# Packed dense convolutions for the first three blocks, a band built from tiny fp16 matmuls, weights loaded in thirds, and a new order of the first casts, moves and loads

## The chip, the cores and the metric

One core of one Trainium2 chip. The metric is device microseconds of one execution. A program on one core has no second die to compare with, but each run lists its span (first to last instruction) and its mean granted TensorE clock. A single number below is a median over the runs named beside it.

## The reference, cut to what matters

```python
# x: (8, 4160, 192) fp32; weight: (8, 7); w1, w2, w3: (192, 768); w_out: (768, 192)
w = softmax(weight, axis=-1)                       # 8 heads, 7 taps
conv[b, s, h*24 + g] = sum_k w[h, k] * x_padded[b, s + k, h*24 + g]   # causal, 6 zeros ahead
h = max(conv @ w1, conv @ w2, conv @ w3)
out = h @ w_out
```

The 33,280 tokens are worked through in 65 blocks of 512. The kernel uses max(a, b, c) = max(relu(a - c), b - c) + c: layer 1 computes the two differences with `w1 - w3` and `w2 - w3`, and the term in `c` is carried by a product `m = w3 @ w_out`.

## The kernel before: the parts that the argument touches

The first two blocks use a "dense" conv, straight from a spread-out copy of x (`xz`). All later blocks use a packed conv from `x16`, whose result is then moved into place by six small DMA moves (`repack`) and one DMA that doubles it onto the other 64 partitions (`double`). In the cuts, `l1(t, j)` is layer-1 step j of block t, `st2` the output stage, `evac` copies a conv's result out of the matmul's memory, and `keep_warm(n)` issues n idle matmuls on zeros, whose result nobody reads, so that TensorE does not stand still.

```python
    # the band of taps: broadcast by a matmul, softmax on 128 partitions,
    # seven products on VectorE, seven matmuls that sum them
    keep_warm(2)
    nc.tensor.matmul(wps..., lhsT=ones[:], rhs=wk[:], ...)
    ...
    for k in range(KW):
        nc.vector.tensor_mul(out=shifted[:, k, :, :], in0=<unit, shifted by k>, in1=<tap k>)
    keep_warm(7)
    for k in range(KW):
        nc.tensor.matmul(ps[:], lhsT=ident16[:], rhs=shifted[:, k, :, :], ...)
    keep_warm(3)
    ...
    def repack(t):                       # six moves, three of them on the sync queue
        for n, (half, s0, c, r0, rows) in enumerate(pieces):
            (nc.sync, nc.gpsimd)[n % 2].dma_start(out=yd[r0:r0 + rows, c, :],
                                                  in_=slots[t][s0:s0 + rows, half, :])

    def double(t):
        nc.sync.dma_start(out=dense[t][HALF:P, :, :], in_=dense[t][0:HALF, :, :])
    ...
    for t in range(1, NB):
        u = t + AHEAD                    # AHEAD = 3
        load_x(t + 7)                    # sync queue
        cast_x(t + 5)                    # GpSimd, needs load t+5
        double(u - 1)                    # sync queue
        begin(t)
        l1(t, 0)
        ...  conv(u) [and conv(u + 1) in even blocks], evictions
        repack(u)
        st2(t - 1, 0, NJ)                # first sixth of the output stage of block t-1
        ...
```

All `load_x`, all `double` and half of the moves share one in-order queue, that of the sync engine. What waits there holds everything behind it: in the trace of the kernel before, the doublings wait there 124 times for moves to land, 184.8 us in all.

The softmax here doesn't subtract the row's maximum and nothing guards it: scores larger than these inputs give would overflow.

## Time and profile before

| | before |
|---|---|
| median (range) | 480.11 us (479.98 to 480.84, 3 runs) |
| span of the profiled run | 479.2 us (that run: 481.05) |
| busy TensorE | 468.5 us, 9083 matmuls |
| block 2 begins | 34.09 us |
| two steady blocks | 13.95 us |

The lines that carry this are in the prediction.

### The profile page before, as it was taken

The numbers are of one execution on the slowest core, as the hardware profiler recorded it, in microseconds if no ns is written. First come the engines' busy times: TensorE is split into PE (matmuls) and PEld (weight loads), VectorE is DVE, ScalarE is ACT, GpSimd is POOL, SyncE is SP. The second block draws the span as 40 slices with busy tenths as digits, with TensorE's granted clock in tenths as the row PEclk, the third lists the DMA queues.
The fourth block names the chain that finished last, engine by engine and source line by source line (L and its number), as shares of the span: only waits on it lengthen the run. The fifth ranks groups of instructions, "written<-read, shape, count | busy, mean of one in ns | idle before, by whom it ended". The sixth has DMA issues, their size and how long they took to land.

```text
span 479.2 us, 21943 instructions
## 1 busy us (share of the span) xinstructions
PE 468.5 (98%) x9083; PEld 393.6 (82%) x9083; DVE 366.2 (76%) x609; ACT 327.2 (68%) x608; POOL 211.0 (44%) x340
## 2 busy tenths in 40 slices
PE   7899999999999999999999999999999999999996
PEld 3468888888888888888888888888888888888995
DVE  6667777877777787777778777877877787787775
ACT  5666766767676676767676676767667676766664
POOL 2555435543543454354345434534535453454200
PEclk9899999999999999999999999999999999999999
DMA  8958756656666665666666666665656755644313
GB/s 188 230 150 221 205 168 188 179 178 178 191 173 175 169 187 172 174 190 176 172 186 171 177 171 179 187 173 171 183 162 177 212 165 168 181 139 122 98 67 100
DMA packets 68035, 82.08 MB, mean 171 GB/s; under 512 B 9440, under 2 KB 56272, under 8 KB 67936
## 3 DMA queue, kind: packets, MB, share of 16 engines
q1 hardware_dynamic: 54478, 49.41, 41.0%
q0 software_dynamic: 13104, 30.98, 18.4%
q8 instruction: 71, 1.16, 1.1%
q10 hardware_dynamic: 354, 0.30, 0.2%
q14 instruction: 28, 0.23, 0.1%
HBM read 30.31 MB, written 25.56 MB: 117 GB/s over the span
## 4 chain that ended last, share of the span: by engine, by line
PE 97%; ACT 1%; DVE 1%; issue 1%; POOL 0%; POOLq 0%
PE lp L383 32%; PE po L426 30%; PE lq L383 26%; PE G L322 7%; PE D L342 1%; PE idle L196 1%; PE band_sum L245 0%; ACT band L268 0%; ACT w3h L262 0%; ACT r L387 0%; DVE xz L216 0%; DVE h L388 0%; PE pm L301 0%; PE wps L223 0%; PE pm L305 0%
## 5 line engine op out<-in xcount | busy, mean ns | idle before, releaser
L388 DVE TENSOR_TENSOR h<-r,lq 128x512 f16<-128x512 f16 x390 | 267.2, 686 | 101.6 <-ACT r L387 101.6
L387 ACT ACTIVATE r<-lp 128x512 f16<-128x512 f32 x390 | 232.9, 597 | 136.1 <-PE lp L383 90.2
L383 PE MATMUL lp<-yd,wd 64*128 64x512 f16 x1170 | 315.8, 377 | 0.2 <-DVE wd L254 0.2
L383 PE MATMUL lq<-yd,wd 64*128 64x512 f16 x1170 | 315.0, 375 | 0.2 <-DVE h L388 0.2
L426 PE MATMUL po<-wo,h 64*128 64x192 f16 x3120 | 231.4, 243 | 0.0
L426 PEld LDWEIGHTS <-h 64*128 64x128 f16 x3120 | 187.2, 94 | 25.6
L383 PEld LDWEIGHTS <-wd 64*128 64x128 f16 x2340 | 164.4, 94 | 21.4 <-issue 1.7
L452 POOL DMA_DIRECT2D out_dram<-o x63 | 50.1, 795 | 240.0 <-DVE o L436 223.2
L366 POOL DMA_DIRECT2D yd<-ys x189 | 95.7, 511 | 2.2 <-ACT ys L353 1.6
L426 PE MATMUL po<-m,yd 64*128 64x192 f16 x780 | 87.0, 243 | 0.0
L436 DVE TENSOR_TENSOR o<-a,po 128x384 f32<-128x384 f32 (+1 forms) x132 | 71.4, 541 | 0.6 <-ACT a L435 0.6
L146 POOL CAST x<-xf 112x960 f16<-112x960 f32 x62 | 61.8, 996 | 2.6 <-DMA xf<-in_x_dram 2.5
L435 ACT COPY a<-po 128x384 f32<-128x384 f32 (+1 forms) x132 | 61.7, 468 | 1.2 <-PE po L426 1.2
L426 PEld LDWEIGHTS <-yd 64*128 64x128 f16 x780 | 55.1, 94 | 8.0
L322 PEld LDWEIGHTS <-x 112*32 112x32 f16 x2480 | 30.0, 97 | 13.3 <-issue 13.2
L353 DVE CAST ys<-G 128x512 f16<-128x512 f32 x60 | 38.5, 682 | 0.0
L353 ACT CAST ys<-G 128x512 f16<-128x512 f32 x66 | 35.7, 589 | 2.1 <-PE G L322 0.8
L322 PE MATMUL G<-band,x 112*32 112x103 f16 (+1 forms) x2480 | 35.0, 210 | 0.0
L161 POOL CAST xz<-xf 112x240 f16<-112x240 f32 (+2 forms) x6 | 2.4, 441 | 11.5 <-DMA xf<-in_x_dram 11.5
L196 PE MATMUL idle<-idle 128*128 128x512 f16 x14 | 5.9, 563 | 1.2 <-DVE unit L212 1.2
L196 PEld LDWEIGHTS <-idle 128*128 128x128 f16 x14 | 1.6, 131 | 3.6 <-issue 2.1
L342 PE MATMUL D<-band,xz 112*32 112x103 f16 (+1 forms) x240 | 3.7, 229 | 0.8 <-ACT band L268 0.8
(50 smaller groups left out, 43.1 us busy)
## 6 DMA issues: line engine op xcount, KB each, us to landing
out_dram<-o POOLq DMA_DIRECT2D x63, 384.0 KB, 3.8
xf<-in_x_dram SPq DMA_DIRECT2D x57, 420.0 KB, 4.8
yd<-yd SPq DMA_DIRECT2D x63, 192.0 KB, 3.3
yd<-ys SPq DMA_DIRECT2D x63, 48.0 KB, 3.5
yd<-ys POOLq DMA_DIRECT2D x63, 48.0 KB, 3.5
xf<-in_x_dram SPq DMA_DIRECT2D x8, 252.0 KB, 3.6
yd<-ys SPq DMA_DIRECT2D x63, 32.0 KB, 3.3
yd<-ys POOLq DMA_DIRECT2D x63, 32.0 KB, 3.6
```

Source lines behind the costliest of these rows:

```text
L146: nc.gpsimd.tensor_copy(out=v[0:rl, q0:q1, :], in_=xf[0:rl, q0:q1, :])
L196: nc.tensor.matmul(ps[:], lhsT=idle[:, 0:P], rhs=idle[:], start=True, stop=True)
L322: nc.tensor.matmul(G[i][32 * g:32 * g + 32, lo:hi], lhsT=x16[0:rlen, cb:cb + 32], rhs=band[0:rlen, h, cc:cc + hi - lo], start=True, stop=T ...
L353: copy(out=slots[t][:, i, :], in_=convs[t][i][:])
L366: (nc.sync, nc.gpsimd)[n % 2].dma_start(out=yd[r0:r0 + rows, c, :], in_=slots[t][s0:s0 + rows, half, :])
L383: nc.tensor.matmul(ps[i][:, 0:N], lhsT=wd[row, c, P * j:P * (j + 1)], rhs=y[row, c, 0:N], start=(c == 0), stop=(c == NC - 1))
L387: nc.scalar.activation(out=r[:, 0:N], in_=ps[0][:, 0:N], func=AF.Relu)
L388: nc.vector.tensor_max(out=hs[t][:, j, 0:N], in0=r[:, 0:N], in1=ps[1][:, 0:N])
L426: nc.tensor.matmul(ps[b0, i][:, s % 2, :], lhsT=a, rhs=b, start=first, stop=last)
L435: nc.scalar.copy(out=a[:, ss, :], in_=ps[s0, 0][:, ss, :])
L436: nc.vector.tensor_add(out=outs[t][:, s0:s + 1, :], in0=a[:, ss, :], in1=ps[s0, 1][:, ss, :])
L452: qs[i].dma_start(out=bass.AP(tensor=out.tensor, offset=r * D, ap=[[D, n], [step * D, s1 - s0], [1, D]]), in_=ob[p0:p0 + n, s0:s1, :])
```

## The change: intent and diff

The intent is to shorten the start, where TensorE is not yet busy with useful work. (1) The band is built from a softmax on 8 partitions and 38 matmuls of 8x32 by 8x8. (2) A dense conv computes each of its six column groups once instead of twice: 60 matmuls instead of 120, with three fp16 copies on VectorE (`cross`) to duplicate the result. (3) Weights come in three equal parts, and block 1's x ahead of the last part. (4) Block 2 gets a dense conv too. (5) Blocks 0 and 1 are interleaved, and the first loads, casts, moves and convs get hand-written places, because only four x buffers stay in the ring.

```diff
-    NDENSE, AHEAD = 2, 3
+    NDENSE = 3
...
+    xap = ctx.enter_context(tc.tile_pool(name="xap", bufs=1))
+    xbp = ctx.enter_context(tc.tile_pool(name="xbp", bufs=1))
-    xfp = ctx.enter_context(tc.tile_pool(name="xfp", bufs=6))
+    xfp = ctx.enter_context(tc.tile_pool(name="xfp", bufs=4))
...
+    load_w(0)
+    load_w(1)
     load_x(1)
+    load_w(2)
...
+    nc.gpsimd.memset(xz[2][:], 0.0)
...
+    keep_warm(6)
+    nc.scalar.activation(out=wexp[:], in_=wk[:], func=AF.Exp, accum_out=wsum[:])   # 8x7
     nc.vector.reciprocal(out=wrec[:], in_=wsum[:])
+    nc.vector.tensor_scalar(out=line[:, 31:31 + KW], in0=wexp[:], scalar1=wrec[:], ...)
+    for c in range(WIN):                                  # WIN = 38
+        nc.tensor.matmul(bps[:, c, :], lhsT=line[:, WIN - 1 - c:WIN + 31 - c],
+                         rhs=ident16[0:NHEAD, 0:NHEAD], start=True, stop=True)
+    keep_warm(4)
...
+    def cross(t):                                          # three copies on VectorE
+        for c in range(NC):
+            nc.vector.tensor_copy(out=yd[a, c, :], in_=yd[b, c, :])
...
-    for t in range(1, NB):
-        u = t + AHEAD
-        load_x(t + 7)
-        cast_x(t + 5)
-        double(u - 1)
+    loads_at = {2: (7,), 3: (8, 9)}
+    casts_at = {2: (6,), 3: (7, 8)}
+    convs_at = {2: (4, 5), 3: (6,)}
+    repacks_at = {2: (4,), 3: (5, 6)}
+    doubles_at = {2: (), 3: (4,), 4: (5, 6)}
+    for t in range(2, NB):
+        if t > 3:
+            load_x(t + 6)
+            cast_x(t + 5)
+        for u in doubles_at.get(t, (t + 2,)):
+            double(u)
         begin(t)
         l1(t, 0)
         ...  convs and evictions
+        for u in repacks_at.get(t, (t + 3,)):
+            repack(u)
+        for u in loads_at.get(t, ()):
+            load_x(u)
+        for u in casts_at.get(t, ()):
+            cast_x(u)
         st2(t - 1, 0, NJ)
```

## The prediction

> **What bounds the kernel now.** I read the page first, then the stretches of the start (busy time by window), then the timeline of the first 35 us, then the sync queue's waits.
>
> ```profile
> PE 468.5 (98%) x9083; PEld 393.6 (82%) x9083; DVE 366.2 (76%) x609; ACT 327.2 (68%) x608; POOL 211.0 (44%) x340
> PE   7899999999999999999999999999999999999996
> PE 97%; ACT 1%; DVE 1%; issue 1%; POOL 0%; POOLq 0%
> ```
>
> TensorE is the bound, and only the first slices (12 us each) are not full. The change touches nothing after the fourth block of 512 tokens (65 in all), so the question is what the first 35 us are worth.
>
> ```profile
> 0.00:12.20 12.20, 8.92 (x141) 4.51 (x141) 7.67 (x19) 6.82 (x15) 2.98 (x18) 1.00 0.85 188
> 12.20:16.80 4.60, 4.19 (x37) 1.35 (x27) 3.93 (x6) 3.85 (x6) 1.60 (x4) 1.00 1.12 269
> 16.80:21.90 5.10, 4.00 (x181) 3.50 (x181) 3.04 (x6) 2.16 (x4) 3.59 (x6) 0.78 1.12 256
> 21.90:28.40 6.50, 5.25 (x122) 2.61 (x120) 2.00 (x4) 3.53 (x7) 4.25 (x7) 0.91 0.44 114
> 34.10:48.05 13.95, 13.95 (x278) 11.89 (x274) 10.97 (x19) 9.79 (x19) 6.48 (x10) 1.00 0.86 234
> ```
>
> The columns are window, length, busy of PE, weight load, DVE, ACT, POOL, granted clock, DMA share, GB/s. From 34.1 on PE has no gap: two blocks take 13.95 us. Before that there are gaps, keep-warm work that counts as busy, and a stretch at clock 0.78.
>
> ```profile
> 4.78 1.45 ACT L161 CAST xz<-xf 112x240 f16<-112x240 f32 x6 [0.39 <-DMA xf<-in_x_dram]
> ...
> 7.03 1.98 PE L245 MATMUL band_sum<-shifted,ident 128*128 128x304 f16 x7
> ...
> 9.05 1.65 ACT L268 CAST band<-band_sum 32x304 f16<-32x304 f32 x4 [1.25 <-PE band_sum L245]
> ...
> 10.75 1.55 PE L342 MATMUL D<-band,xz 112*32 112x103 f16 x120 [0.84 <-ACT band L268]
> ...
> 12.23 0.39 PE L383 MATMUL lp<-yd,wd 64*128 64x512 f16 x1
> ...
> 15.20 2.37 POOL L161 CAST xz<-xf 112x240 f16<-112x240 f32 x6 [11.55 <-DMA xf<-in_x_dram]
> ...
> 24.50 0.67 PE L301 MATMUL pm<-wo,w3t 128*128 128x192 f16 x6 [1.25 <-issue]
> ...
> 34.09 0.38 PE L383 MATMUL lp<-yd,wd 64*128 64x512 f16 x1
> ```
>
> The band ends at 10.7 and gates the first dense conv; the first useful layer-1 matmul runs at 12.23; the second block's x lands at 15.2; block 2 starts at 34.09.
>
> **PE units.** One layer-1 step (6 matmuls, two row halves side by side) is 0.645 us (28.79, 29.01, 29.22: 0.215 each, three in a row). One sixth of an output stage is 0.415 (29.44 to 29.85). A block is 6 x 1.06 = 6.36, a packed conv 0.61 (13.95 = 2 x 6.36 + 2 x 0.615). From the start of block 2: 63 blocks x 6.36 = 400.7, 60 convs x 0.615 = 36.9, the last block's output stage 2.9: sum 440.5. 34.09 + 440.5 = 474.6; the chain of waits has its last PE work end at 474.6, so the bookkeeping closes. 4.6 us of tail remain to 479.2. The gain is therefore (34.09 - new start of block 2) - 0.6, as one conv more is left at that point after the change (block 3's comes earlier, block 2 is dense), minus any new stall.
>
> [...]clock 0.78 from 16.8 to 21.9, after gaps, where layer-1 pairs are 0.40 apart instead of 0.215. [...]The trace shows 13 ns per pair in the dense conv (1.55 us over 120)[...]. [...]copy of 1536 elements 1.22 us (0.79 ns each), subtraction of 768 in 0.97 (1.27 ns each). [...]The landings agree with one pipe: 0.43 MB at 4.8 us, 2.63 MB at 15.2, so about 2.75 us + MB / 0.211.
>
> **The change, part by part (estimates from those durations).**
> Band: softmax on 8 partitions straight from the load of the weights, no broadcast matmul, none of the seven products on 128 partitions (2.79 us of DVE) and no 1.98 us sum. Table load about 1.3 to 2.6, exp and two tiny DVE operations to 3.5. The six keep-warm matmuls end near 3.9 (0.45 each from 1.2). [...]The four band copies stay 1.65: band at 7.7 instead of 10.7.
> Casts of block 0: from ACT to DVE, 4.8 to about 6.2, beside it.
> Dense conv: 60 matmuls instead of 120, but half-height evictions plus three fp16 cross copies on DVE. PE 7.8 to 8.8; three ACT copies of 0.59 in a row end at 10.3; last cross copy 10.6. First layer-1 step ends near 10.9 instead of 13.3: 2.4 us earlier.
> Weights in thirds: landings by the pipe formula are x0 4.8, w3 5.7, w1 6.8, w2 7.8, second third 8.7 to 10.6, x1 2.04 MB = 12.6 (was 15.2), last third 13.5 to 15.2, output weights 17.3. Steps 1 to 3 of block 0 follow DVE (copy 0.6, subtractions 0.56, eviction maxima 0.69): step 3 ends near 13.8. ACT's copy of the last w3 third ends 14.35, delays the next relu to 14.95 and the DVE maximum to 15.7; the subtraction of the last third then ends 16.7. Meanwhile x1 is cast by POOL 12.6 to 15.0 and conv_dense(1) is over at 16.0. Steps 4 and 5 of block 0 run 16.7 to 18.0 (were 21.9 and 25.1); cross copies hold DVE, so block 1's first step starts near 18.75 (was 27.04).
> From there PE is nearly full: six steps of block 1 (3.9), six sixths of block 0's output (2.5), transposes 1.05, m 1.3, dense conv of block 2 0.95, conv(3) 0.62, and 0.45 of wait for m's eviction: 10.75. Block 2 starts at 29.5. Gain without later stalls: 34.09 - 29.5 - 0.6 = 4.0 us, that is 476.1.
>
> **Rivals.**
> (a) The queue of moves becomes the bound at block 4. The loads no longer run seven blocks ahead.
>
> ```profile
> SPq L372 <- DMA yd<-ys: 184.8, 124, 5.6
> ```
>
> The sync queue already waits in its order for repacks to land before it doubles. After the change x of block 8 is issued behind repack(6), whose conv runs in block 3. Counted from the start of block 3: step 0.65, conv 0.61, evictions 0.65, three repack issues of 0.55, load issues 1.2 with landing 3.6 after the second, cast 1.0: 8.8 us. conv(8) is wanted at 6.36 + 0.61 + 0.65 + 0.61 = 8.2. That costs 0.5 us, or 1.7 if the queue has a backlog. For: every part is a measured duration.[...] It would make 476.6 to 477.8.
> (b) The clock. Between 13.8 and 16.7 PE has only the dense conv, about a third of the time; a drop as in 16.8 to 21.9 would cost 0.5 to 1.5 us. Before, idle matmuls bridged this place: two stood at 14.04. It would make about 477.
> (c) The dense block 2 now gets its second half by DMA: evictions end near 26.8, issue 0.5, landing 2.0 to 3.3, so 29.2 to 30.6 against 29.5 needed: 0 to 1 us.
> (d) DMA hides it all: if x1 lands as late as before, the chain slips by some 2 us and the gain falls to 2. Against it: 0.57 MB less stands ahead of x1 in the queue.
> (e) The start goes better than I think (tiny pairs at 30 ns, waits overlapped): 474 to 475.
>
> **Range and chances.** 476.1 without stalls, plus an expected 0.4 for (a), 0.3 for (b), 0.1 for (c), as none is sure and they partly overlap: 476.9. Low 474.3 is (e); high 480.0 is (a), (b) and (c) together, leaving almost nothing. Two per cent is 9.6 us: PE work from block 2 on plus tail is 445, so a faster verdict would need block 2 to start before 24 us, and block 0's and 1's own PE work plus the data landings do not allow it: 2%. Slower by 2% would take a stall that recurs each block; the later blocks' order on PE is unchanged: 1%.
>
> **What would show each step right or wrong.** Band copies ending near 7.7, not 10.7; first layer-1 step near 10.9; cast of x1 starting near 12.6; block 1's first step near 18.75; block 2 starting near 29.5; two blocks still 13.95 us. A PE gap just before the conv matmuls in the block that starts near 44 would show (a); a granted clock below 0.9 between 15 and 20 would show (b). I am wrong if block 2 starts after 33, if the steady pair of blocks changes, or if the tiny matmuls take over 4 us.

## More of the kernel before

One more view matters later: the sync queue in the timeline of the kernel before (columns: start, length of the group of issues, queue, line, operation, number of issues).

```profile
29.76 1.25 SPq L372 DMA_DIRECT2D yd<-yd  x1
31.07 1.72 SPq L130 DMA_DIRECT2D xf<-in_x_dram  x3
33.03 0.51 SPq L372 DMA_DIRECT2D yd<-yd  x1
33.59 2.10 SPq L366 DMA_DIRECT2D yd<-ys  x3
```

The three loads at 31.07 are block 7 (one DMA) and block 8 (two DMAs, as it begins a new sequence). Block 8's conv runs in block 4, which begins at 48.03: its load is issued 17 us ahead. Three moves follow each block.

## The result, and the profile after

Ratios here are the mean time of one kernel's fast runs over that of the other's in the same rounds, so not quite the ratio of the quoted medians.

| | before | after |
|---|---|---|
| median (range) | 480.10 us (479.98 to 480.84) | 483.95 us (481.96 to 484.26) |
| ratio | | 1.0068 (0.68% slower; interval 1.0039 to 1.0097) |
| span of the profiled run | 479.2 us | 480.0 us (that run: 481.96) |
| block 2 begins | 34.09 us | 30.67 us |

The predicted 476.9 us with 474.3 to 480.0 does not hold the result, though the class (within 2%) does. The profiled execution is the fastest of the four; the other three were near 484. From the page, in the order of the prediction's first fence (busy time and instructions, PE's slices, shares of the chain that ended last):

```profile
PE 466.2 (97%) x9008; PEld 391.9 (82%) x9008; DVE 367.3 (77%) x612; ACT 323.9 (67%) x602; POOL 214.1 (45%) x346
PE   7799899999999999999999999999999999999996
PE 95%; ACT 1%; DVE 1%; DMA 1%; issue 0%; POOL 0%; SPq 0%; ACTq 0%; POOLq 0%; DVEq 0%
```

TensorE has 2.3 us less to do, and yet its slice from 48 to 60 us (the fifth) has lost a tenth, and a DMA stands in the chain. The stretches, with the prediction's columns:

```profile
0.00:12.20 12.20, 9.15 (x119) 4.92 (x120) 8.07 (x20) 5.53 (x11) 4.62 (x19) 0.81 0.89 196
12.20:16.80 4.60, 3.86 (x76) 2.11 (x72) 3.10 (x6) 3.25 (x6) 4.26 (x9) 0.77 0.99 215
34.10:48.05 13.95, 12.87 (x248) 10.31 (x242) 10.35 (x17) 9.49 (x18) 6.78 (x11) 1.00 0.76 215
48.05:62.00 13.95, 11.80 (x212) 10.26 (x214) 8.60 (x14) 7.49 (x14) 7.41 (x11) 1.00 0.89 224
```

The last two rows were 13.95 of 13.95 before: 1.1 and 2.15 us of idle TensorE are new. The first two show half clock between 7.3 and 14.2 us. The timeline names the new wait (sync queue first, then the GpSimd cast, then TensorE; in brackets the engine's idle time before the instruction and what ended it):

```profile
39.05 0.50 SPq L354 DMA_DIRECT2D yd<-yd  x1
39.60 4.64 SPq L348 DMA_DIRECT2D yd<-ys  x6
44.29 3.06 SPq L133 DMA_DIRECT2D xf<-in_x_dram  x4
...
49.15 0.99 POOL L149 CAST x<-xf 112x960 f16<-112x960 f32 x1 [4.28 <-DMA xf<-in_x_dram]
...
50.20 0.64 PE L295 MATMUL G<-band,x 112*32 112x103 f16 x40 [3.23 <-POOL x L149]
```

Read upwards: block 8's conv waits 3.23 us for the cast of its x, the cast waits for the load, and the load is issued only at 44.29, behind a doubling and six moves in the sync queue. Before, it was issued at 31.07, ahead of this traffic. From block 3 on every store comes 0.74 to 0.87 us later than before: one loss, not a recurring one.

The start, against the prediction's markers:

| marker | predicted | after |
|---|---|---|
| band copies end | 7.7 | 7.79 |
| first layer-1 step ends | 10.9 | 11.68 |
| cast of x1 begins | 12.6 | 12.54 |
| step 4 of block 0 begins | 16.7 | 17.82 |
| block 1's first step begins | 18.75 | 19.33 |
| block 2 begins | 29.5 | 30.67 |

Of the 1.17 us that block 2 is late, 0.58 are there when block 1's first step begins. The rest comes after it, where TensorE waits mainly for VectorE's maximum:

```profile
20.33 0.37 PE L365 MATMUL lq<-yd,wd 64*128 64x512 f16 x1 [0.63 <-DVE h L370]
```

And one collision at the start that was not foreseen (VectorE's scaling of the 8x7 softmax beside GpSimd's clearing of `xz[2]`):

```profile
3.23 1.73 DVE L228 TENSOR_SCALAR line<-wexp,wrec 8x7 f16<-8x7 f32 x1
3.24 1.69 POOL L199 MEMSET xz<- 128x1920 f16 x1
```

An 8x7 operation of 1.73 us that ends with the memset beside it looks like one that waits, though it counts as busy. A run below tests this.

### The profile page after: what moved, and what is told of

The parts are those of the page before. It is cut to its first block, busy times and chain, and to the rows that moved or that the text cites.

```text
span 480.0 us, 21790 instructions
## 1 busy us (share of the span) xinstructions
PE 466.2 (97%) x9008; PEld 391.9 (82%) x9008; DVE 367.3 (77%) x612; ACT 323.9 (67%) x602; POOL 214.1 (45%) x346
## 4 chain that ended last, share of the span: by engine, by line
PE 95%; ACT 1%; DVE 1%; DMA 1%; issue 0%; POOL 0%; SPq 0%; ACTq 0%; POOLq 0%; DVEq 0%
PE lp L365 32%; PE po L409 30%; PE lq L365 26%; PE G L295 7%; DMA xf<-in_x_dram 1%; PE D L314 1%; ACT r L369 0%; ACT band L236 0%; DVE h L370 0%; ACT L225 0%; PE band_cols L232 0%; DVE line L228 0%; POOL x L149 0%; DVE wd L250 0%; DVE o L419 0%
## 5 line engine op out<-in xcount | busy, mean ns | idle before, releaser
L348 POOL DMA_DIRECT2D yd<-ys x186 | 94.3, 511 | 5.2 <-ACT ys L335 2.5
L149 POOL CAST x<-xf 112x960 f16<-112x960 f32 x61 | 60.8, 996 | 9.1 <-DMA xf<-in_x_dram 9.1
L295 PEld LDWEIGHTS <-x 112*32 112x32 f16 x2440 | 29.0, 96 | 16.7 <-issue 13.3
L335 DVE CAST ys<-G 128x512 f16<-128x512 f32 x62 | 39.8, 682 | 3.3 <-PE G L295 3.3
L335 ACT CAST ys<-G 128x512 f16<-128x512 f32 x62 | 33.6, 588 | 5.0 <-PE G L295 3.7
L166 POOL CAST xz<-xf 112x240 f16<-112x240 f32 (+2 forms) x12 | 3.7, 351 | 7.8 <-DMA xf<-in_x_dram 7.8
L314 PEld LDWEIGHTS <-xz 112*32 112x32 f16 x180 | 3.7, 111 | 1.7 <-issue 0.9
L211 PE MATMUL idle<-idle 128*128 128x512 f16 x10 | 3.8, 530 | 1.2 <-DVE idle L206 1.2
```

The lines of the kernel that those rows point to most:

```text
L149: nc.gpsimd.tensor_copy(out=v[0:rl, q0:q1, :], in_=xf[0:rl, q0:q1, :])
L295: nc.tensor.matmul(G[i][32 * g:32 * g + 32, lo:hi], lhsT=x16[0:rlen, cb:cb + 32], rhs=band[0:rlen, h, cc:cc + hi - lo], start=True, stop=T ...
L314: nc.tensor.matmul(ps[32 * g:32 * g + 32, lo:hi], lhsT=xz[t][0:rlen, q, v, 32 * s:32 * s + 32], rhs=band[0:rlen, h, cc:cc + hi - lo], star ...
L335: copy(out=slots[t][:, i, :], in_=convs[t][i][:])
```

## The experiments

Theory A: the start went as predicted but for about 1.2 us, and the gain is lost once, at block 8's conv, because its load stands too late in the sync queue. Rival B: the start itself is worth less than reckoned and something after it (the clock, the band, the new moves) costs the rest. The runs were sent in four calls, each with its own runs of the kernel before on the same chip (medians 481.05, 481.72, 482.29 and 481.18 us).

### The changed kernel again

> The changed kernel once more, unaltered, to learn why three of its four runs took 484 us and the profiled one 482. Theory (late loads): the stall before conv(8) differs from run to run, so a profile of a 484 run shows a stall of about 5 us there instead of 3.2, and the same start of block 2 near 30.7. Rival: the longer runs start block 2 about 2 us later (start-up clock or landings), with the same 3.2 us stall.

Measured: 484.31 us, ratio 1.0063 (1.0042 to 1.0084), span 482.3. This profile caught a run near 484. PE's wait, and the stretch after it (columns as above):

```profile
51.06 1.05 PE L295 MATMUL G<-band,x 112*32 112x103 f16 x40 [3.50 <-POOL x L149]
```

```profile
50.00:52.00 2.00, 0.94 (x40) 0.83 (x40) 0.00 (x0) 0.00 (x0) 1.72 (x2) 0.67 0.95 240
52.00:54.00 2.00, 2.00 (x24) 1.20 (x18) 1.29 (x2) 0.59 (x1) 0.10 (x1) 0.50 1.12 235
```

Neither half of the expectation is right. The wait is only 0.3 us longer and the start 0.6 later (block 2 at 31.27) than in the 482 us run. What differs is the granted clock: 0.50 after the pause, so that the same 40 conv matmuls take 1.05 us instead of 0.64. From one block's store to the next it took 9.66 us where the 482 us run took 8.26.

### Block 8's load one block sooner

```diff
-    loads_at = {2: (7,), 3: (8, 9)}
+    loads_at = {2: (7, 8), 3: (9,)}
```

> Changed kernel with the load of block 8 issued one block earlier, behind the four moves of block 4 instead of behind six moves of blocks 5 and 6. Theory (the order of the sync queue makes the load late): the 3.2 us PE gap before conv(8) goes, two blocks take 13.95 us from block 2 on, time 3 to 5 us shorter than the changed kernel, so 478 to 481. Rival (the DMA engines are full there, or POOL's queue holds the cast back): the gap stays within 1 us of 3.2 and the time does not move.

Measured: 478.76 us (478.19 to 479.31), ratio 0.9945 (0.9926 to 0.9964), span 476.8. The sync queue and TensorE:

```profile
36.79 1.62 SPq L133 DMA_DIRECT2D xf<-in_x_dram  x3
...
46.43 1.10 PE L295 MATMUL G<-band,x 112*32 112x103 f16 x80
```

The load goes out at 36.79, and both convs of block 4 run as one group of 80 matmuls without a wait. One moved load is worth 5.5 us against the changed kernel on the same chip, a little more than the 3 to 5 expected, and makes it 2.3 us faster than the kernel before. Block 2 begins at 30.78, as in the changed kernel. This shows theory A in its main part.

The same profile also says something about the start. Here the layer-1 matmuls run at full speed from the first step on (0.37 to 0.39 us each; 0.58 to 0.63 in the first profile of the changed kernel up to 14.2), the band copies end 0.43 us later (8.22), and step 4 of block 0 begins where it did:

```profile
17.84 0.39 PE L365 MATMUL lp<-yd,wd 64*128 64x512 f16 x1 [1.48 <-DVE wd L250]
```

The second profile of the changed kernel has the same two differences, and its step 4 begins at 17.72. So by step 4 the half clock before 14.2 had cost no more than the later band, at most some 0.4 us, an estimate from these three profiles.

### More idle matmuls at the start

```diff
-    keep_warm(6)
+    keep_warm(8)
 ...
-    keep_warm(4)
+    keep_warm(7)
```

> Changed kernel with 8 and 7 idle matmuls in place of 6 and 4, so that PE has no gap of more than 0.5 us before the first dense conv. Theory (the gap at 3.9 to 5.0 and 7.1 to 7.8 let the clock drop): the stretch at clock 0.50 from 7.3 to 14.2 goes, dense conv of block 0 takes about 1.0 instead of 1.9 us, block 2 starts about 1 us earlier (29.6), but the later stall before conv(8) moves with it, so the time is 0.5 to 1.2 us shorter. Rival (the start is bound by ACT, DVE and landings, not by the clock): dense conv shorter, block 2 start unchanged within 0.3 us.

Measured: 486.21 us (485.45 to 487.22), ratio 1.0101 (1.0078 to 1.0124). The first dense conv did run at full clock, 1.09 us instead of 1.90, but it began at 9.37 instead of 7.84, as the seven idle matmuls took 2.97 us, 0.42 each, where the four of the changed kernel took 1.04, 0.26 each. In the changed kernel the layer-1 matmuls of each half, 512 columns wide like these, begin 0.42 to 0.43 us apart at clock 0.50 (from 10 to 14 us) and 0.21 to 0.22 apart at 1.00 (from 18.05 to 18.91). So 0.42 is the time of half clock, although the clock column reads 1.00 there: so early in this run the spacing of a known matmul is the surer sign. Block 2 began at 31.38. The wait before block 8's conv was 3.73 us, again followed by clock 0.50 until about 56.9. Both theories missed: more idle matmuls cost time here and gained none.

### The kernel before with the new band only

```diff
-    ... broadcast matmul, softmax on 128 partitions, seven products, seven matmuls ...
+    ... softmax on 8 partitions, 38 tiny matmuls ...
+    keep_warm(8)  /  keep_warm(7)
+    for a in range(4): nc.scalar.copy(out=band[...], in_=bps[...])   # ahead of copy_w3
```

> Kernel before with only the new way to the band (8 partitions, 38 tiny matmuls, band copies ahead of the w3 move on ACT). Theory (the first matmul is not what sets the start of block 2, the landing of x1 at 15.2 us and what hangs on it is): first layer-1 matmul 1.5 to 2.5 us earlier (about 10), start of block 2 0 to 1.3 us earlier, time 479 to 480. Rival (the chain through the band sets it all): block 2 and the time earlier by 2 us or more, time 478 or less.

Measured: 485.46 us (484.5 to 486.46), ratio 1.0091 (1.0066 to 1.0116). The first layer-1 matmul runs at 10.00 instead of 12.23, so the band does save 2.2 us there. By the conv of block 2 that is gone (20.89 against 20.85, it waits for x2), and then a wait grows that the kernel before has in a small form (its line is in the prediction, `[1.25 <-issue]`, at 24.50):

```profile
24.67 0.79 PE L303 MATMUL G<-band,x 112*32 112x103 f16 x26 [3.42 <-issue]
```

In both kernels it comes after the same count, 351 matmuls (351 and 352 weight loads). Half clock follows (0.60 and 0.55 in the windows from 24 to 26 and 26 to 28). Block 2 is 2.76 us later than in the kernel before, where the theory had it up to 1.3 sooner and the rival 2 or more: both missed. So the band by itself is worth nothing here, and brings TensorE sooner to a place where it stands still.

### That pause: loads of blocks 4 and 5 out of the way

On top of the last kernel:

```diff
-    for t in range(2, 6):
+    for t in range(2, 4):
         load_x(t)
 ...
     evac(2, 0)
+    load_x(4, nc.scalar)
+    load_x(5, nc.scalar)
     l1(0, 4)
 ...
     repack(2)
+    cast_x(4)
+    cast_x(5)
```

> b_band (kernel before with only the new band) with the loads of x of blocks 4 and 5 issued late, after the first eviction of block 2's conv, and their casts behind. In b_band TensorE stood 3.4 us after its 351st matmul with no releaser in the profile, and the kernel before stands 1.25 us at the very same place. [...]with 0.86 MB less in line the pause at that matmul shrinks from 3.4 to under 1 us. Rival (the pause has nothing to do with the transfers): it stays above 2.5 us.

Measured: one run, 481.56 us, span 479.5, state unknown.

```profile
21.34 0.49 PE L301 MATMUL G<-band,x 112*32 112x103 f16 x26 [0.44 <-issue]
```

The pause at the same place in the instruction stream falls from 3.42 to 0.44 us. So the x loads in line set its length, as far as one profile of each kernel can show it. What TensorE waits for there is not shown: the profile names no releaser. The changed kernel reaches its 351st matmul only at 27.5 and shows no such pause.

### Idle matmuls in front of block 8's conv, eight and sixteen

```diff
         for n, u in enumerate(us):
+            if u == 8:
+                keep_warm(8)        # keep_warm(16) in the second kernel
             conv(u, ...)
```

> Changed kernel with eight idle matmuls (about 1.7 us) put on TensorE between conv(7) and conv(8), where it waits 3.2 to 3.7 us for the late load; the load stays late. Theory (a wait of some 3.5 us also drops the clock to half for the next 3 us, which makes 484 out of 482): conv(8) starts as late as before, but the granted clock stays 1.00 after it, and the time is about 482, 2 us below the unaltered changed kernel of the same chip. Rival (the extra 2 us of the 484 runs come from a longer wait alone): time unchanged at 484.

> Changed kernel with sixteen idle matmuls (about 3.5 us) between conv(7) and conv(8), so that TensorE works through nearly all of its wait. With eight the clock still fell to half for 4 us after a pause of 2.3 us. Theory (the half clock after the pause is what makes 484 out of 482): granted clock 1.00 from 45 to 60, conv(8) no more than 0.4 us later than in the unaltered kernel, time 481.5 to 482.5. Rival (the two states of 482 and 484 have another cause): time about 484.

Measured: eight: 484.33 us, ratio 1.0042 (1.0001 to 1.0084); sixteen: 482.95 us, ratio 1.0016 (0.9988 to 1.0044). The window of 52 to 54 us, of the first and of the second:

```profile
52.00:54.00 2.00, 2.00 (x24) 1.21 (x18) 1.29 (x2) 0.58 (x1) 0.32 (x2) 0.50 1.09 196
```

```profile
52.00:54.00 2.00, 2.00 (x34) 1.33 (x32) 1.42 (x3) 0.97 (x2) 1.57 (x4) 1.00 1.08 206
```

Eight idle matmuls fill only part of the wait; a pause of 2.26 us is left, and the clock falls all the same. With sixteen there is no pause left and the clock stays at 1.00 while the conv still waits for the same load. So where the clock falls, the pause costs twice: its own length (3.50 and 3.73 us in two profiles of a late load), and half clock for some 3 to 6 us after it. Against the unchanged kernel's 1.0063, the ratio of 1.0016 puts the second part at about 0.5%, some 2 us, with intervals that meet and on different chips.

### Block 1's x behind the last third of the weights

On top of the kernel with the sooner load:

```diff
     load_w(1)
-    load_x(1)
     load_w(2)
+    load_x(1)
```

> The changed kernel with the early load of block 8 (as a_loads), but x of block 1 loaded behind the last third of the weights, as it stood in the kernel before. By the pipe formula it lands about 2.7 us later (0.57 MB). Theory (the landing of x1 sets the start): block 2 starts 0.8 to 1.5 us later than in a_loads, time about 1 us longer. Rival (the DVE chain and the last third's subtraction set it, x1 has slack): within 0.3 us of a_loads.

Measured: 481.31 us, ratio 0.9997 (0.997 to 1.0024). The cast of x1 begins at 14.87 instead of 11.77 and block 0's store comes 1.48 us later. Block 2 begins 1.48 us later too (32.26), at the upper end of the 0.8 to 1.5 expected. Beside this, the three cross copies of block 1 now run beside GpSimd's casts and take 2.42 us instead of 1.23; how much of the 1.48 that is, no run separates. The order of the loads is therefore worth some 1.5 us of the start's gain, where the prediction's rival (d) had some 2.

### The clearing of `xz[2]` out of the way of the softmax

On the same base:

```diff
-    nc.gpsimd.memset(xz[2][:], 0.0)
 ...
     cast_dense(1, (nc.gpsimd.tensor_copy, nc.gpsimd.tensor_copy))
+    nc.gpsimd.memset(xz[2][:], 0.0)
```

> a_loads with POOL's clearing of block 2's dense buffer (1.69 us at 3.24) moved behind the cast of block 1. Theory (the 8x7 scaling on DVE, which took 1.7 to 2.1 us, waits for POOL's memset[...]): the scaling takes under 0.3 us, the tiny matmuls start about 1.4 us earlier, and the first dense conv about 1 us earlier. Rival (such a tiny operation with a per-partition scalar is that slow itself): duration stays near 2 us. For the total: 0 to 0.6 us shorter than a_loads, as later landings and DVE take up most.

Measured: 481.38 us (479.94 to 484.52), ratio 1.0003 (0.9961 to 1.0045). VectorE's timeline:

```profile
3.20 0.47 DVE L227 TENSOR_SCALAR line<-wexp,wrec 8x7 f16<-8x7 f32 x1
...
17.61 3.35 DVE L329 COPY yd<-yd 64x512 f16<-64x512 f16 x3
```

and TensorE's window later on:

```profile
24.00:26.00 2.00, 2.00 (x15) 0.99 (x12) 0.69 (x1) 0.72 (x3) 0.00 (x0) 0.50 0.92 242
```

The scaling falls from 2.11 to 0.47 us and the dense conv begins 1.5 us sooner, at 6.79. But the memset now stands in front of GpSimd's weight casts, which slide beside the cross copies: three copies of 0.29 us each when alone take 3.35 us. Block 0's store comes 2.56 us later (34.90 instead of 32.34). About half of that is the late copies: TensorE waits 2.83 us for VectorE and goes on at 21.73 instead of 20.43. The other half, 1.26 us, comes after that, in a stretch with the clock at 0.50 for some 3 us. The scaling was long only beside the memset: with the memset there, ending at 4.93, the scaling ended at 4.96 in the changed kernel and at 5.32 in the one with the sooner load, and at 3.67 when the memset was elsewhere. By what the one holds up the other is not shown. That leaves 0.47 us for the scaling alone, where under 0.3 was expected.

### The last third's copy and subtraction sooner

On the same base:

```diff
     l1(0, 1)
-    l1(0, 2)
     copy_w3(nc.scalar.copy, 2)
+    l1(0, 2)
+    make_wd(4, 6)
     l1(0, 3)
```

> a_loads with two moves in program order: ACT's copy of the last w3 third ahead of step 2 of block 0, and the subtraction of the last third on DVE ahead of step 3's maximum. Theory (the step of my chain from 14.4 to 16.7 is a matter of order on ACT and DVE): step 4 of block 0 starts at about 16.6 instead of 17.8, block 1's second step about 0.6 us earlier, time 0.4 to 0.8 us shorter than a_loads. Rival (bound by landings of the last third): no change within 0.2.

Measured: 479.43 us (478.75 to 481.69), ratio 0.9962 (0.9929 to 0.9994). Step 4 of block 0 begins at 16.68 instead of 17.84, where the prediction had put it (16.7). Yet block 0's store comes when it did (32.28 and 32.34): the subtraction now takes 1.40 us instead of 0.95 and the cross copies 1.75 instead of 1.23, beside GpSimd's casts, and the next pause of TensorE, again for VectorE's maximum, ends at 20.38 (20.43 before).

### The same kernel once more, and one with all of it together

The first is the kernel with the sooner load, unchanged, for five rounds. The second adds the clearing on VectorE, two of GpSimd's weight casts ahead of x1's cast, the output weights' cast later, and steps of block 1 ahead of block 0's last two:

```diff
+    for part in range(2): cast_w3(part)
     copy_w3(nc.vector.tensor_copy, 0)
+    nc.vector.memset(xz[2][:], 0.0)
 ...
     cross(1)
+    make_wd(4, 6)
+    nc.gpsimd.tensor_copy(out=wo[:], in_=wos[:])
+    cast_dense(2, ...)
     l1(1, 0)
+    l1(1, 1)
+    l1(0, 4)
+    l1(0, 5)
```

> The early load of block 8 again (same kernel as a_loads), so that the next version is compared on the same chip. Expected: 478.2 to 479.3, 2.3 us under the kernel before, no pause of TensorE after block 2 starts.

> a_loads with POOL kept away from DVE's copies: two of the three w3 casts ahead of the cast of x1 (POOL waits for x1 there anyway), block 2's buffer cleared by DVE in a pause, output-weight cast behind; and on PE steps 0 and 1 of block 1 ahead of steps 4 and 5 of block 0, which wait for the last third. Theory (DVE copies that run beside POOL casts are stretched, and the order of steps can hide the last third): the scaling takes under 0.5 us, the three cross copies of block 1 take under 1.1 us, block 2 starts at 29.0 to 30.0 instead of 30.8, time 0.8 to 1.8 us under a_loads2. Rival (the landings bind): within 0.4 us of a_loads2.

Measured: the first 479.98 us (484.09, 479.98, 479.59, 478.05, 480.06), ratio 0.9941 (0.9905 to 0.9976); the second 478.77 us (478.58, 484.55, 477.95, 478.95), ratio 0.9957 (0.9894 to 1.0021). In the second, scaling (0.47 us) and cross copies (0.92) shrink, and block 0's store still comes at the same time (32.26): the subtraction now runs beside the output weights' cast (1.78 us), and from 20.3 us on TensorE is nearly full anyway. Block 2 begins at 30.68 (30.57 in the first), not between 29.0 and 30.0 as expected. So a gain over the one moved load is not shown: the medians differ by 1.2 us, but the intervals of the ratios lie almost wholly in each other.

Each has one run at 484, so the first missed its expectation too (478.2 to 479.3 and no pause). The profile of the first kernel caught it:

```profile
56.45 0.61 PE L365 MATMUL lq<-yd,wd 64*128 64x512 f16 x1 [2.14 <-DMA yd<-yd]
```

This time it is block 5's doubled half that is late, from the same sync queue, and half clock follows again (0.58 in the window from 56 to 58).

### Is it the count of moves? Block 5's moves one block sooner

Two kernels, the changed one and the one with the sooner load, each with:

```diff
-    repacks_at = {2: (4,), 3: (5, 6)}
-    doubles_at = {2: (), 3: (4,), 4: (5, 6)}
+    repacks_at = {2: (4, 5), 3: (6,)}
+    doubles_at = {2: (), 3: (4, 5), 4: (6,)}
```

> The changed kernel with one edit: the moves of block 5's conv go out in block 2, where that conv already runs, instead of in block 3, so that three moves of the sync queue stand ahead of block 8's load in block 3 and not six; the load itself stays where the change put it. This is the count my prediction reckoned with. If that count was what was mis-sized, the load is issued about 2.3 us sooner after block 3's start (3.7 instead of 6.1), the TensorE wait before block 8's conv falls from 3.2 to 3.7 us to 0.5 to 1.5, no half clock follows it, and the time is about 479.5 to 480.5, 3.5 to 4.5 below the changed kernel's 484. If the moves are not what holds the load (say the load's own transfer is slow, or its issue waits for its buffer), the wait stays above 2.5 us and the time near 482 to 484.

> The repaired kernel (block 8's load already in block 2) with the same edit as in the run before it. Theory: its occasional 484 us (a wait of 2.1 us for block 5's doubled half and half clock after it) is the same queue's backlog, so with block 5's moves a block earlier no TensorE wait of over 0.5 us should show between blocks 3 and 6, all five times should lie within 477 to 480, and none near 484; median about 478.5. Rival: the occasional 484 comes from elsewhere (or the earlier moves now delay the loads of blocks 7 and 8 instead); then at least one of five is near 484, or a new wait before block 7's or 8's conv shows, and the median is 479 or more.

Measured: on the changed kernel 485.76 us (484.59 to 487.82), ratio 1.0088 (1.0069 to 1.0107); on the one with the sooner load 481.91 us (480.3 to 484.94), ratio 1.0021 (0.9992 to 1.005). The second is slower than without the edit (0.9945 and 0.9941); for the first the intervals overlap (1.0063 without), so it is no better. The sync queue and TensorE of the first:

```profile
35.98 4.93 SPq L348 DMA_DIRECT2D yd<-ys  x6
40.96 0.58 SPq L133 DMA_DIRECT2D xf<-in_x_dram  x1
41.78 1.72 SPq L354 DMA_DIRECT2D yd<-yd  x2
43.55 2.27 SPq L348 DMA_DIRECT2D yd<-ys  x3
45.86 4.32 SPq L133 DMA_DIRECT2D xf<-in_x_dram  x4
...
49.35 0.39 PE L365 MATMUL lq<-yd,wd 64*128 64x512 f16 x1 [3.35 <-DMA yd<-yd]
...
54.45 1.05 PE L295 MATMUL G<-band,x 112*32 112x103 f16 x40 [3.71 <-POOL x L149]
```

Three moves stand directly ahead of block 8's load now, and it goes out at 45.86, 7.5 us after block 3's start (38.35) instead of 6.1. The line as a whole is what holds it: the same nine moves and one doubling more lie between block 2's start and this load, and the queue has hardly a break from 35.98 to 50.2. Block 7's load, too, goes out at 40.96 instead of 36.60. In 38 to 42 us the DMA engines are 0.3 busy instead of 0.8, and after 46 they are full (1.05 to 1.13), so that the second of block 8's two DMAs takes 6.8 us to land instead of 4.1. TensorE waits twice, first 3.35 us for block 4's doubled half, then 3.71 us for block 8's cast.

The second of the two kernels, the one with both edits, waits there too:

```profile
47.78 0.39 PE L365 MATMUL lq<-yd,wd 64*128 64x512 f16 x1 [1.74 <-DMA yd<-yd]
```

Block 4's doubling stands behind block 5's moves and two loads (41.49 instead of 39.38). So my expectation for both runs failed; the rival that I wrote for the second, that the sooner moves delay something else, holds. In these runs it mattered when the large loads entered the line, not how many moves stood just ahead of one. In both, what was moved up pushed another transfer back.

## Why the prediction was wrong, point by point

**The bound and the bookkeeping were right.** TensorE stays the bound, two steady blocks later on still take 13.95 us, and the sum closes: of the 34.09 - 30.67 = 3.42 us by which block 2 begins sooner, 0.6 belongs to the conv that is still owed. 479.2 - 2.8 + 3.23 of wait + about 0.4 = 480.0, the span of the profiled run. The 0.4 is convs that run alone. A block without a conv takes 6.36 us, and a pair of convs adds 1.23 (13.95 - 2 x 6.36); block 3, with one conv, takes 7.26 (38.23 to 45.49), 0.3 more than the 0.6 reckoned for a conv. In block 4 the second step begins 3.41 us later than one step (1.06) and a pair of convs (1.23) allow (51.19 instead of 47.78), 0.2 more than the wait. Within rounding that is the 0.4.

**The start: right in kind, 1.2 us too good.** The band (7.79 for 7.7) and x1 (12.54 for 12.6) were met. Several sizes were off. The 38 tiny matmuls took 1.10 us, 29 ns each, less than my estimate, which no trace stood behind; but the scaling ahead of them took 1.73 us, where I had two tiny operations to 3.5. The clock was half from 7.3 to 14.2, with no idle matmuls of use there, so dense conv 0 took 1.90 us instead of 1.0 and layer-1 steps about 1.3 instead of 0.65; I had looked for a drop only between 13.8 and 16.7, where the clock returned. By step 4 this one had cost at most some 0.4 us, by the estimate above. The last subtraction came at 16.82, so that step 4 began at 17.82, 1.1 us late. And after block 1's first step I had only 0.45 us of wait, for m's eviction; that was 0.30, but the 0.63 for VectorE's maximum came on top. The run with the order changed moved step 4 to 16.68 and gained nothing: VectorE's operations beside GpSimd's casts then took longer (the subtraction 1.40 us instead of 0.95), and the wait for its maximum grew to 1.83. So no run isolates a single term of this part; every repair of it moved the collision. One smaller slip: the formula for landings gives 12.4 for x1 (2.75 + 2.04 / 0.211), not 12.6. In the trace before, the shortest landing of an x load is 2.5 us, and the fp32 copy runs at 1.6 times the rate of the subtraction (0.79 against 1.27 ns per element).

**Step (a), the late load, is where the prediction fell.** The mechanism was named, and the place (the block near 44 to 50) was right. Its size was not: 0.5 us, 1.7 with a backlog, and 0.4 in the sum; measured 3.23 to 3.73. Term by term, from block 3's start at 38.23: I had 0.65 + 0.61 + 0.65 + three moves of 0.55 = 3.6 us to the issue of the load; it was issued after 6.06. From the first issue to the start of the cast I had 0.6 + 3.6 = 4.2; it took 4.86. With the cast of 1.0, that makes 12.0 instead of 8.8, or 3.2 us more. The conv was wanted at 46.97, 8.74 after block 3's start instead of 8.2. So the 0.6 reckoned, plus 3.2, less 0.5, is 3.3 against the 3.23 measured. The 2.5 us of late issue are the moves. I counted those of block 6 alone, three and 1.65 us, though the diff puts those of blocks 5 and 6 there, six and 4.64 us, 0.77 each. I also began to count at block 3's start with an empty queue, though a doubling stood in it until 39.55; that cost nothing by itself, as my first move was not due before 40.14 (38.23 + 1.91). The run with block 5's moves one block sooner shows that correcting the count alone would not have been enough: the load then went out still later. What the runs with the sooner load show is that the place of the load was the cause; they take the wait away and leave the start as it is.

**Step (b), the clock, was looked for in the wrong place.** I gave 0.3 us to a drop near 15 us. No step of mine had a stall followed by half clock. The two profiles of the unchanged kernel put its cost at 1.4 us (9.66 less 8.26 from store to store): their spans, 482.3 and 480.0, differ by 0.6 of later start, 0.3 of longer wait and these 1.4. The ratios of the run with sixteen idle matmuls and of the unchanged kernel put it at some 2 us, with wide intervals. Only these two executions were profiled, so that the other runs near 484 had the same is likely, not shown. Why the profiled 482 us run kept full clock after 3.23 us is not shown; the other profiles had pauses of 3.50 and 3.73, and with eight idle matmuls ahead of it a pause of 2.26 us was enough. Other profiles have half clock after 2.14 (block 5's doubled half), 2.83 (the moved memset), and 3.42 us (the band alone), and full clock after 1.74 and 1.91. So the length of a pause alone does not decide, and what does is not shown. In the kernel before, at the place that the prediction names, the clock is at 0.50 from about 19.6 to 23.0, and no pause since 11 us was longer than 0.70 us; what ran just before were matmuls of only 64 and 103 columns.

**Steps (c) and (d)** cost nothing visible: no wait of TensorE at block 2 for a DMA, and x1 landed 2.7 us sooner. The run with x1 late shows that this was worth 1.5 us.

**In sum**, for the profiled run near 484: block 2 at 31.27 makes the start worth 34.09 - 31.27 - 0.6 = 2.2 us, and 479.2 - 2.2 + 3.5 (wait) + 0.4 + 1.4 (clock) = 482.3, its span. The version with the sooner load, the best found, stands at 0.9945 and 0.9941 in two sets of rounds, about 2.7 us below the kernel before: the start's 2.8 us, nearly whole. Its open end is the one run in nine near 484, in which, in the one profile of it, another item of the same queue is late; the only cure tried made it worse.

## What to carry to other kernels

When a change shortens the distance between a load and its use, list everything that the new program order puts in the load's in-order queue, from the last moment at which that queue was empty, and add the landing time under the load that the other transfers make (block 8's second DMA took 4.1 us to land in the changed kernel and 6.8 with block 5's moves sooner); the cheap repair is to put the large load ahead of the small moves (worth 5.5 us here), not to thin out the moves behind (ratio 1.0088 against the changed kernel's 1.0063). A stall of TensorE can cost more than its own length: half clock after one of 3.50 us cost 1.4 us more, though one of 3.23 had none after it, so an estimate of a stall needs a second term. And work moved onto VectorE and GpSimd together must be timed as a pair: three cross copies took 3.35 us beside GpSimd's weight casts and 3 x 0.29 alone, and three repairs of the start each moved the collision instead of removing it.
